# Attention in steps of whole tiles instead of half tiles, ahead of a routed feed-forward layer, on one core

## The chip, the core and the metric

The kernel is one program on one core of a Trainium2 chip. The core has TensorE (matrix products), VectorE, ScalarE, GpSimd and SyncE (here a queue that issues transfers), which run their own instructions in order and wait for each other by semaphores. The metric is device time in microseconds, the median of three runs. One execution was also taken with a profile.

## The reference

Attention over 4 batches of 8 heads, 768 rows, 64 columns a head, feeds a mixture of 8 experts with a fixed capacity and then a two-layer network:

```python
scores = scale * np.matmul(q, k.transpose(0, 1, 3, 2))
is_global = pos[None, :] < n_global              # 8
is_local = (rel >= 0) & (rel < n_local)          # 96
keep = is_global | is_local
dist = np.where(is_global & ~is_local, n_local, np.abs(rel))
scores = np.where(keep, scores - slopes * dist, -1e9)
a = np.exp(scores - scores.max(-1)); a = a / (a.sum(-1) + 1e-9)
x = np.matmul(a, v)      # rows of all heads side by side: 3072 x 512
x = moe(x)               # greedy routing by x @ w_gate, 8 experts of 384 rows
out = (relu-like(x @ w_in)) @ w_out
```

[...]

## The kernel before

The attention goes by 24 tiles of 128 rows (6 to a batch). A tile `g` sees 8 global columns, the 96 before it and its own 128: 232 columns (`KW`); the first tile of a batch sees 128. A tile is worked in two halves of 4 heads, so there are 48 half steps. The order of all instructions is written out by hand, and each engine runs its own in that order. In half step `n` come: the scores of the **next** half (`scores`: 4 products on TensorE; on VectorE the bias and the negative maximum in one instruction a head, L199, called a lift in what follows; on ScalarE the exponential with its sum, L202), the transposes of this half's weights (`transpose_p`: part 0 the own 128 columns, copied to SBUF by VectorE, L217; part 1 the columns before, copied by ScalarE, L215), the combination of the half **two** before (`combine`: a product that turns the values' result back to rows and gives the router's logits, L261, and on VectorE L247, L270, L280, L283), and the values of the half before (`values`, L232, whose result VectorE copies in half 0, L238, and ScalarE in half 1, L236). The columns before a tile end in the tile before, so the values of part 1 are the tile before's `a_v`, into whose first 32 rows GpSimd copies the global values (`place_values`, L177).

Beside this run 32 jobs of `Doubles`, one a half step in four of five (`turn`). A job has raw words of 128x512 weights. *Begin* (at the start of a half step): SyncE issues the load of the job after next (L67), ScalarE makes absolute values (L72) and scales the low words (L74), GpSimd clamps (L73) and then finishes the job before, in every second job with L86 and L87. *Join* (at the end): VectorE shifts (L78) and puts the sign bit in (L79), GpSimd adds the low words (L81). The router's constant tables (`setup`) are made piece by piece, one piece a half step.

After the last `combine` comes the routing of the first expert, then 8 experts on TensorE; that part is the same in both kernels.

Of the kernel before, what the change touches and what calls it, by code (L numbers as in the profile page):

```python
# [30 lines left out]
class Doubles:  # L31
# [58 lines left out]
def attention(ctx, tc, q, k0, k, v, w_gate, n_global, n_local, ident, x_dram, logits, side, router):  # L90
# [43 lines left out]
    vg = consts.tile([C - W, 2, H, D], FT, name="a_vg")  # L134
    pbuf = consts.tile([C, 4, 2, 2 * C], FT, name="a_p")
# [27 lines left out]
    nc.gpsimd.memset(vg, 0.0)  # L163
    nc.gpsimd.memset(cmb, 0.0)
    nc.gpsimd.memset(pbuf[:, :, :, :C - GW], 0.0)
# [7 lines left out]
    def place_values(g, u):  # L173
        b, t = divmod(g, NT)
        if t:
            hs = slice(4 * u, 4 * u + 4)
            nc.gpsimd.tensor_copy(T["v", g - 1][:C - W, hs], vg[:, b % 2, hs])  # L177

    def scores(g, u):
        b, t = divmod(g, NT)  # L180
        if t:
            n, bs = KW, bias
        else:
            n, bs = C, bias0
        ps = [psum.tile([C, 2, KW], FT, name=f"a_s{s}", bufs=2) for s in range(2)]
        if u == 0:
            T["sum", g] = work.tile([C, H], FT, name="a_sum", bufs=3)
            T["mn", g] = work.tile([C, H], FT, name="a_mn", bufs=3)
        for a in range(2):
# [4 lines left out]
        for a in range(2):  # L194
            sx = work.tile([C, 2, KW], FT, name="a_sx", bufs=2)
            pr = T["P", g, 2 * u + a] = pbuf[:, 2 * u + a]
            for s in range(2):
                h = 2 * (2 * u + a) + s
                nc.vector.tensor_tensor_reduce(out=sx[:, s, :n], in0=ps[s][:, a, :n], in1=bs[:, h], scale=-scale,  # L199
                                               scalar=BIG, op0=OP.add, op1=OP.min,  # L200
                                               accum_out=T["mn", g][:, h:h + 1])
                nc.scalar.activation(pr[:, s, 2 * C - n:], sx[:, s, :n], AF.Exp, bias=T["mn", g][:, h:h + 1],  # L202
                                     scale=-1.0, accum_out=T["sum", g][:, h:h + 1])

    def transpose_p(g, u, part):
# [3 lines left out]
        ps = psum.tile([C, 4, C], FT, name=f"a_pt{part}")  # L209
        sb = work.tile([C, 4, C], FT, name=f"a_pts{part}", bufs=2)  # L210
        for i in range(4):
            pr = T["P", g, 2 * u + i // 2][:, i % 2]
            nc.tensor.transpose(ps[:, i], pr[:, :C] if part else pr[:, C:], ident)  # L213
# [4 lines left out]
        T["PT", g, u, part] = sb  # L218

    def values(g, u):  # L220
        t = g % NT
        if g == NG - 1 and u:
            ps = psum.tile([C, 2, KW], FT, name="a_s0", bufs=2)[:, :, :C]
        else:
            ps = psum.tile([C, 2, C], FT, name="a_xp")
# [8 lines left out]
        xt = work.tile([C, 2, C], FT, name="a_xt", bufs=2)  # L234
        if u:
            nc.scalar.activation(xt, ps, AF.Copy)  # L236
        else:
            nc.vector.tensor_copy(xt, ps)  # L238
        T["xt", g, u] = xt

    def divisor(g, u):
        e = T["se", g, u] = work.tile([C, 4], FT, name="a_se", bufs=4)
        nc.gpsimd.tensor_scalar(e, T["sum", g][:, 4 * u:4 * u + 4], 1e-9, None, op0=OP.add)

    def norm(g, u):
        r = T["r", g, u] = rows.tile([C, 4], FT, name="a_r")
        nc.vector.reciprocal(r, T.pop(("se", g, u)))  # L247
# [4 lines left out]
    def combine(g, u):  # L252
        xt = T.pop(("xt", g, u))
# [6 lines left out]
        for a in range(2):  # L260
            nc.tensor.matmul(ps[:, a], xt[:, a], cmb[:, 2 * u + a], start=True, stop=True)  # L261
# [3 lines left out]
        if not last:  # L265
            norm(g, u)
        r = T.pop(("r", g, u))
# [14 lines left out]
        if u:  # L282
            nc.vector.tensor_reduce(logits[:, g, :], T["lp", g].rearrange("c h e -> c e h"), axis=AX.X, op=OP.add)  # L283
            if g < NG - 2:
                T["store"] = g
            else:
                store(g)

    def turn(n):
        return 2 <= n < N - 3 and n % PACE[1] < PACE[0]  # L290

    NG = B * NT
    steps = [(g, u) for g in range(NG) for u in range(2)]
    N = len(steps)
    scores(0, 0)
    setup = router.setup()
    for n in range(N + 2):
        if n < N:
            g, u = steps[n]
            if u == 1 and g + 3 < NG:  # L300
                load_kq(g + 3)
            if u == 1 and g + 2 < NG:
                load_v(g + 2)
            if "store" in T:
                store(T.pop("store"))
            nx = steps[n + 1] if n + 1 < N else None
# [941 lines left out]
```

## Time and profile before

| | us |
|---|---|
| median of 3 runs | 1077.29 (1076.77 to 1078.17) |
| the profiled execution | 1076.5 |
| its span, first to last instruction | 1074.7 |
| TensorE busy in the span | 1032.3 |
| VectorE busy | 739.1 |
| ScalarE busy | 380.3 |
| GpSimd busy | 559.5 |
| mean granted clock of TensorE | 0.986 of full |

A busy time is a share of a span with very different stages: the attention fills the first 197 us, the experts the rest. The granted clock is a share of TensorE's full clock.

### The profile page before, as it was taken

The numbers are of one execution on the slowest core, as the hardware profiler recorded it, in microseconds if no ns is written. First come the engines' busy times: TensorE is split into PE (matmuls) and PEld (weight loads), VectorE is DVE, ScalarE is ACT, GpSimd is POOL, SyncE is SP. The second block draws the span as 40 slices with busy tenths as digits, with TensorE's granted clock in tenths as the row PEclk, the third lists the DMA queues.
The fourth block names the chain that finished last, engine by engine and source line by source line (L and its number), as shares of the span: only waits on it lengthen the run. The fifth ranks groups of instructions, "written<-read, shape, count | busy, mean of one in ns | idle before, by whom it ended". The sixth has DMA issues, their size and how long they took to land.

```text
span 1074.7 us, 19352 instructions
## 1 busy us (share of the span) xinstructions
PE 1032.3 (96%) x6475; PEld 908.8 (85%) x6475; DVE 739.1 (69%) x2215; ACT 380.3 (35%) x958; POOL 559.5 (52%) x867
## 2 busy tenths in 40 slices
PE   8888989789999999999999999999999999999997
PEld 6766767569888988898899888988998999999996
DVE  7999999787878787877887788678855313231322
ACT  6788878233224311331233123312321232124211
POOL 5867876055668434643564346433742464247223
PEclk9999999799999999999999999999999999999999
DMA  8677774152254336335433643543354335335141
GB/s 287 221 243 262 269 268 156 31 150 77 98 193 151 127 109 215 99 109 175 157 93 106 208 136 98 163 151 119 99 175 139 120 124 189 118 118 167 60 136 70
DMA packets 86771, 160.80 MB, mean 150 GB/s; under 512 B 9584, under 2 KB 42864, under 8 KB 86672
## 3 DMA queue, kind: packets, MB, share of 16 engines
q1 hardware_dynamic: 82832, 146.98, 41.3%
q0 software_dynamic: 3840, 12.59, 3.5%
q8 instruction: 51, 0.84, 0.3%
q14 instruction: 48, 0.39, 0.1%
HBM read 138.57 MB, written 20.97 MB: 148 GB/s over the span
## 4 chain that ended last, share of the span: by engine, by line
PE 74%; DVE 6%; POOL 3%; issue 3%; DMA 1%; ACT 1%; POOLq 0%; DVEq 0%; ACTq 0%
PE m_h L983 22%; PE m_acc L1028 22%; PE m_acc L970 12%; PE m_h L943 11%; POOL m_g L912 1%; PE a_xp L232 1%; PE a_pt L213 1%; POOL m_so L912 1%; PE a_s L193 1%; DMA m_x<-x_rows,r_idx 1%; PE m_h L869 1%; ACT a_p L202 1%; DVE r_red L795 1%; PE a_cb L261 1%; DVE a_sx L199 1%
## 5 line engine op out<-in xcount | busy, mean ns | idle before, releaser
L912 POOL TENSOR_TENSOR m_g<-m_t,m_g 128x192 fp32r<-128x192 f32 (+1 forms) x286 | 163.7, 594 | 335.6 <-ACT m_g L992 335.0
L1028 PE MATMUL m_acc<-m_so,m_g 128*128 128x512 f32 x1143 | 294.0, 398 | 0.0
L983 PE MATMUL m_h<-m_y,wi 128*128 128x384 f32 x1536 | 290.1, 339 | 0.0
L983 PEld LDWEIGHTS m_h<-m_y,wi 128*128 128x128 f32 x1536 | 267.4, 188 | 6.6 <-DVE m_xt L885 0.2
L1028 PEld LDWEIGHTS m_acc<-m_so,m_g 128*128 128x128 f32 x1143 | 209.2, 189 | 34.5 <-POOL m_g L912 0.5
L912 POOL TENSOR_TENSOR m_s<-m_r,m_s 128x256 fp32r<-128x256 f32 x256 | 187.3, 755 | 77.5 <-ACT m_s L902 77.2
L992 ACT ACTIVATE m_g<-m_t 128x384 fp32r<-128x384 f32 (+1 forms) x143 | 70.0, 489 | 427.0 <-DVE m_t L991 249.1
L990 DVE TENSOR_SCALAR m_t<-m_h,m_al 128x384 f32<-128x384 f32 (+1 forms) x144 | 82.3, 571 | 155.7 <-PE m_h L983 145.4
L970 PE MATMUL m_acc<-m_hh,m_s 128*128 128x384 f32 x768 | 148.0, 339 | 0.0
L943 PE MATMUL m_h<-m_xt,m_s 128*128 128x384 f32 x768 | 144.4, 336 | 0.6 <-DVE m_xt L885 0.4
L943 PEld LDWEIGHTS m_h<-m_xt,m_s 128*128 128x128 f32 x768 | 134.5, 188 | 2.4 <-DVE m_xt L885 0.6
L970 PEld LDWEIGHTS m_acc<-m_hh,m_s 128*128 128x128 f32 x768 | 132.7, 189 | 0.0
L902 ACT ACTIVATE m_s<-m_r 128x512 fp32r<-128x512 f32 x128 | 79.7, 626 | 68.4 <-PE m_acc L970 66.7
L202 ACT ACTIVATE a_p<-a_sx,a_mn 128x232 f32<-128x232 f32 (+1 forms) x192 | 88.4, 462 | 38.2 <-DVE a_mn L199 38.2
L947 DVE SCALAR_TENSOR_TENSOR m_hh<-m_h,m_hh 128x384 fp32r<-128x384 f32 x64 | 35.5, 555 | 78.4 <-ACT m_hh L946 78.2
L991 DVE SCALAR_TENSOR_TENSOR m_t<-m_h,m_t 128x384 f32<-128x384 f32 (+1 forms) x144 | 73.9, 513 | 4.9
L795 DVE TENSOR_REDUCE r_red<-r_cmp 128x24 bf16<-128x576 bf16 (+1 forms) x97 | 73.8, 761 | 3.3
L213 PE MATMUL a_pt<-ident,a_p 128*128 128x128 f32 x352 | 57.3, 294 | 15.9 <-DVE a_r L247 13.2
L213 PEld LDWEIGHTS a_pt<-ident,a_p 128*128 128x128 f32 x352 | 39.2, 144 | 36.9 <-ACT a_p L202 23.1
L199 DVE CUSTOM_DVE_ANT_0 a_sx<-a_s,a_bias 128x232 f32<-128x232 f32 (+1 forms) x192 | 61.4, 374 | 4.3 <-PE a_s L193 2.6
L946 ACT ACTIVATE m_hh<-m_h 128x384 fp32r<-128x384 f32 x64 | 31.5, 492 | 91.1 <-PE m_h L943 88.8
L193 PE MATMUL a_s<-a_k,a_q 64*128 64x232 f32 (+1 forms) x384 | 51.0, 388 | 3.6 <-DMA a_q<-in_q_dram 3.6
(192 smaller groups left out, 1162.4 us busy)
## 6 DMA issues: line engine op xcount, KB each, us to landing
m_so<-wo_pairs SPq DMA_DIRECT2D x112, 512.0 KB, 3.5
m_r<-in_moe_w_dram SPq DMA_DIRECT2D x128, 256.0 KB, 3.0
a_k<-in_k_dram SPq DMA_DIRECT2D x20, 464.0 KB, 5.2
f_raw<-in_moe_w_in_dram SPq DMA_DIRECT2D x16, 512.0 KB, 4.0
f_raw<-in_moe_w_out_dram SPq DMA_DIRECT2D x16, 512.0 KB, 5.4
wo_pairs<-m_so SPq DMA_DIRECT2D x16, 512.0 KB, 2.7
a_v<-in_v_dram SPq DMA_DIRECT2D x24, 256.0 KB, 5.1
x_rows<-a_xo SPq DMA_DIRECT2D x24, 256.0 KB, 3.0
```

Of the source, the lines that this page charges most:

```text
L199: nc.vector.tensor_tensor_reduce(out=sx[:, s, :n], in0=ps[s][:, a, :n], in1=bs[:, h], scale=-scale, scalar=BIG, op0=OP.add, op1=OP.min, ac ...
L202: nc.scalar.activation(pr[:, s, 2 * C - n:], sx[:, s, :n], AF.Exp, bias=T["mn", g][:, h:h + 1], scale=-1.0, accum_out=T["sum", g][:, h:h + 1])
L213: nc.tensor.transpose(ps[:, i], pr[:, :C] if part else pr[:, C:], ident)
L795: nc.vector.tensor_reduce(red, cmp, axis=AX.X, op=OP.add)
L902: self.nc.scalar.activation(s[:, 0], r, AF.Copy)
L912: self.nc.gpsimd.tensor_tensor(lo[:, c:c + n], x[:, c:c + n], hi[:, c:c + n], op=OP.subtract)
L943: nc.tensor.matmul(ps[:, :n], s1[:, a, d], x[:, b, d], start=(d == 0 and i == 0), stop=(d == self.ND - 1 and i == 2))
L970: nc.tensor.matmul(ps[:, :n], s2[:, b, d * 128:(d + 1) * 128], h[:, a], start=(f == 0 and a + b == 0), stop=(last and a == 1))
L983: nc.tensor.matmul(ps[:, :n], self.wi[:, a, d, f * 128:(f + 1) * 128], y[:, b, d], start=(d == 0 and i == 0), stop=(d == self.ND - 1 and i ...
L990: nc.vector.tensor_scalar(t[:, cs], ps[:, cs], 0.0, self.al[:, f:f + 1], op0=OP.min, op1=OP.mult)
L991: nc.vector.scalar_tensor_tensor(t[:, cs], ps[:, cs], 0.0, t[:, cs], op0=OP.max, op1=OP.add)
L1028: self.nc.tensor.matmul(self.ex[e]["op"][t], g[:, a, t * 128:(t + 1) * 128], s[:, b], start=(f == 0 and a + b == 0), stop=(f == self.F2 // ...
```

## The change

The loop goes by whole tiles. The scores of both halves of the next tile come first on TensorE, then the transposes of half 0, the combination of half 0 of the tile before, the transposes and the combination of half 1, and at the end the values of both halves into one PSUM bank, which ScalarE copies as a whole. The lifts and the exponentials have functions of their own and are spread between. A tile has two begins and two joins as before, at other places, and the divisor and the reciprocal come once a tile. The weights of a tile have their own buffers (`pbuf` by tile), with 232 columns. The 104 values before a tile (global and local) come as an input of their own, `vw`, laid out by the host, so `place_values` goes. In `join` the sign is masked as 16 bits out of the high word and written into the high half of the low word, which the same addition on GpSimd then adds. The router's tables are made only in half steps without a job, and two copies for them go to ScalarE.

```diff
     def join(self, job):
         nc, t = self.nc, job["t"]
+        parts = job["raw"].bitcast(U16).rearrange("p a (b c) -> p a b c", c=2)
         nc.vector.tensor_scalar(t, t, 3, 0x7FFFFFF8, op0=OP.logical_shift_left, op1=OP.bitwise_and)
-        nc.vector.scalar_tensor_tensor(t, job["raw"][:, :, 1], -0x80000000, t, op0=OP.bitwise_and, op1=OP.bitwise_or)
+        nc.vector.tensor_scalar(parts[:, :, 0, 1], parts[:, :, 1, 1], 0x8000, None, op0=OP.bitwise_and)
...
-        x = T["v", g] = loads.tile([C, H, D], FT, name="a_v", bufs=4)
+        x = T["v", g] = loads.tile([C, H, D], FT, name="a_v", bufs=3)
         nc.sync.dma_start(x, v[b, t * C:(t + 1) * C])
-        if not t:
-            nc.sync.dma_start(vg[C - GW:C - W, b % 2], v[b, :G])
+        if t:
+            x = T["vw", g] = loads.tile([GW, H, D], FT, name="a_vw", bufs=3)
+            nc.sync.dma_start(x, vw[b, t - 1])
-    pbuf = consts.tile([C, 4, 2, 2 * C], FT, name="a_p")
+    pbuf = consts.tile([C, 2, NP, 2, KW], FT, name="a_p")
...
+    def lift(g, p):
+        bs = bias if g % NT else bias0
+        sx = T["sx", g, p] = work.tile([C, 2, KW], FT, name="a_sx", bufs=3)
+        for s, ps in enumerate(T.pop(("S", g, p))):
+            h = 2 * p + s
+            nc.vector.tensor_tensor_reduce(out=sx[:, s, :ps.shape[1]], in0=ps, in1=bs[:, h], scale=-scale,
+                                           scalar=BIG, op0=OP.add, op1=OP.min, accum_out=T["mn", g][:, h:h + 1])
...
-            parts.append((T["v", g - 1], T.pop(("PT", g, u, 1))))
+            parts.append((T["vw", g], T.pop(("PT", g, u, 1))))
...
-        xt = work.tile([C, 2, C], FT, name="a_xt", bufs=2)
-        if u:
-            nc.scalar.activation(xt, ps, AF.Copy)
-        else:
-            nc.vector.tensor_copy(xt, ps)
+        if last:
+            nc.scalar.activation(T["xt", g][:, 2 * u:2 * u + 2], ps, AF.Copy)
+        elif u:
+            nc.scalar.activation(T["xt", g], T["xp"], AF.Copy)
...
+    def turn(n, end=False):
+        if 2 <= n < N - 3 and n % PACE[1] < PACE[0]:
+            next(side)
+        elif end:
+            next(setup, None)
...
+    for g in range(NG):
+        n, ahead, prior = 2 * g, g + 1 < NG, g > 0
+        if g + 3 < NG:
+            load_kq(g + 3)
+        if g + 2 < NG:
+            load_v(g + 2)
+        if g > 1:
+            store(g - 2)
+        turn(n)
+        divisor(g)
+        if ahead:
+            scores(g + 1, 0)
+            scores(g + 1, 1)
+            lift(g + 1, 0)
+            expo(g + 1, 0)
+            lift(g + 1, 1)
+            expo(g + 1, 1)
+            lift(g + 1, 2)
+        transpose_p(g, 0, 0)
+        transpose_p(g, 0, 1)
+        if ahead:
+            lift(g + 1, 3)
+            expo(g + 1, 2)
...
+        if prior:
+            combine(g - 1, 0)
+        transpose_p(g, 1, 0)
+        transpose_p(g, 1, 1)
+        turn(n, True)
+        if ahead:
+            expo(g + 1, 3)
+        if prior:
+            combine(g - 1, 1)
+        turn(n + 1)
+        if not ahead:
+            norm(g)
+        values(g, 0)
+        values(g, 1)
+        turn(n + 1, True)
...
-        nc.vector.tensor_copy(self.tp[:, :, 0], first[:, :, None].to_broadcast([128, U, NB, 2]))
-        nc.vector.tensor_copy(self.tp[:, :, 1], inner[:, :, None, None].to_broadcast([128, U, NB, 2]))
+        for k, t in enumerate((first[:, :, None], inner[:, :, None, None])):
+            nc.scalar.activation(self.tp[:, :, k], t.to_broadcast([128, U, NB, 2]), AF.Copy)
```

## Rows read from the trace of the kernel before

**Rows 1.** Stretches: PE, PEld, DVE, ACT, POOL busy; clock, queue share, GB/s.

```profile
61.50:187.30 125.80, 113.81 (x1062) 88.69 (x1063) 120.07 (x469) 104.97 (x345) 93.38 (x134) 0.97 0.71 244
```

**Rows 2.** The join's two lines: duration min/median/max in ns, first and last start.

```profile
L78 DVE TENSOR_SCALAR f_t<-f_t x32: 415/430/1354, 19.9 to 179.0; 128x512 int32<-128x512 int32 x32
...
L79 DVE SCALAR_TENSOR_TENSOR f_t<-f_raw,f_t x32: 691/693/1651, 20.3 to 179.5; 128x512 int32<-128x512 int32 x32
```

**Rows 3.** VectorE in order of time, about a half tile: start, duration, line.

```profile
71.27 0.27 DVE L283 TENSOR_REDUCE logits<-a_lp 128x8 f32<-128x64 f32 x1
71.45 0.42 DVE L238 COPY a_xt<-a_xp 128x256 f32<-128x256 f32 x1
71.78 0.83 DVE L78 TENSOR_SCALAR f_t<-f_t 128x512 int32<-128x512 int32 x1
...
73.25 0.39 DVE L199 CUSTOM_DVE_ANT_0 a_sx<-a_s,a_bias 128x232 f32<-128x232 f32 x1
...
74.53 0.69 DVE L217 COPY a_pts<-a_pt 128x512 f32<-128x512 f32 x1
75.13 0.17 DVE L247 RECIPROCAL a_r<-a_se 128x4 f32<-128x4 f32 x1
75.41 0.19 DVE L270 TENSOR_TENSOR a_lp<-a_cb,a_r 128x32 f32<-128x32 f32 x1
75.51 0.42 DVE L280 TENSOR_TENSOR a_xo<-a_cb,a_r 128x256 f32<-128x256 f32 x1
75.84 0.42 DVE L78 TENSOR_SCALAR f_t<-f_t 128x512 int32<-128x512 int32 x1
76.30 0.77 DVE L79 SCALAR_TENSOR_TENSOR f_t<-f_raw,f_t 128x512 int32<-128x512 int32 x1
```

**Rows 4.** Joins and their hand-over to and from GpSimd, in order of time.

```profile
35.09 0.62 POOL L73 TENSOR_SCALAR f_t<-f_t 128x512 f32<-128x512 f32 x1
...
35.74 0.43 DVE L78 TENSOR_SCALAR f_t<-f_t 128x512 int32<-128x512 int32 x1
...
36.20 0.98 DVE L79 SCALAR_TENSOR_TENSOR f_t<-f_raw,f_t 128x512 int32<-128x512 int32 x1
...
65.00 0.69 DVE L79 SCALAR_TENSOR_TENSOR f_t<-f_raw,f_t 128x512 int32<-128x512 int32 x1
...
65.83 1.28 POOL L81 TENSOR_TENSOR f_t<-f_t,f_raw 128x512 int32<-128x512 int32 x1 [1.62 <-issue]
```

**Rows 5.** The chain that ended last, where TensorE alone sets it.

```profile
168.33 1.02 PE a_pt L213 x8
...
169.84 1.02 PE a_xp L232 x16
170.87 0.98 PE a_s L193 x8
171.85 1.02 PE a_pt L213 x8
```

**Rows 6.** ScalarE in order of time: exponential, copies, first instruction of a begin.

```profile
75.12 0.47 ACT L202 ACTIVATE a_p<-a_sx,a_mn 128x232 f32<-128x232 f32 x1
...
75.59 0.57 ACT L215 ACTIVATE a_pts<-a_pt 128x512 f32<-128x512 f32 x1
76.07 0.36 ACT L236 ACTIVATE a_xt<-a_xp 128x256 f32<-128x256 f32 x1
76.33 0.68 ACT L72 ACTIVATE f_t<-f_raw 128x512 f32<-128x512 f32 x1
```

**Rows 7.** First lift of tiles 2 and 23, and the last values.

```profile
16.78 0.40 DVE L199 CUSTOM_DVE_ANT_0 a_sx<-a_s,a_bias 128x232 f32<-128x232 f32 x1 [0.38 <-PE a_s L193]
...
187.33 0.40 DVE L199 CUSTOM_DVE_ANT_0 a_sx<-a_s,a_bias 128x232 f32<-128x232 f32 x1 [0.50 <-ACT a_xt L236]
...
195.83 1.04 PE L232 MATMUL a_s<-a_pts,a_v 128*64 128x128 f32 x16
```

**Rows 8.** Loads of the raw weights: count, size, median us from issue to landing.

```profile
f_raw<-in_moe_w_out_dram SPq DMA_DIRECT2D x16, 512.0 KB, 5.4
```

More of the change, by code (lines that the diff above doesn't have):

```diff
@@ L171, in attention @@
     load_v(1)
[L173 to L177, printed above, removed]
-    def scores(g, u):
-        b, t = divmod(g, NT)
-        if t:
-            n, bs = KW, bias
-        else:
-            n, bs = C, bias0
-        ps = [psum.tile([C, 2, KW], FT, name=f"a_s{s}", bufs=2) for s in range(2)]
+    def scores(g, u):
+        n = KW if g % NT else C
         if u == 0:
@@ L188, in scores @@
             T["mn", g] = work.tile([C, H], FT, name="a_mn", bufs=3)
+        ps = [psum.tile([C, 2, KW], FT, name=f"a_s{s}", bufs=2) for s in range(2)]
         for a in range(2):
@@ L193, in scores, with expo @@
                 nc.tensor.matmul(ps[s][:, a, :n], T["q", g][r, p], T["k", g][r, p, :n], start=True, stop=True)
[L194 to L203, printed above, removed]
+            T["S", g, p] = [x[:, a, :n] for x in ps]
+    def lift(g, p):
[5 more added lines that the diff above has]
+                                           scalar=BIG, op0=OP.add, op1=OP.min, accum_out=T["mn", g][:, h:h + 1])
+    def expo(g, p):
+        n = KW if g % NT else C
+        sx = T.pop(("sx", g, p))
+        pr = T["P", g, p] = pbuf[:, g % 2, p]
+        for s in range(2):
+            h = 2 * p + s
+            nc.scalar.activation(pr[:, s, KW - n:], sx[:, s, :n], AF.Exp, bias=T["mn", g][:, h:h + 1],
+                                 scale=-1.0, accum_out=T["sum", g][:, h:h + 1])
     def transpose_p(g, u, part):
@@ L283, in combine @@
             nc.vector.tensor_reduce(logits[:, g, :], T["lp", g].rearrange("c h e -> c e h"), axis=AX.X, op=OP.add)
[L284 to L286 removed]
+            if g >= NG - 2:
                 store(g)
[L289 to L290 removed]
+    def turn(n, end=False):
[3 more added lines that the diff above has]
+            next(setup, None)
     NG = B * NT
[L293 removed]
@@ L294, in attention @@
-    N = len(steps)
+    N = 2 * NG
     scores(0, 0)
-    setup = router.setup()
[L297 to L306, printed above, removed]
-            if turn(n):
-                next(side)
-            if nx:
-                scores(*nx)
-            if n == 0:
-                for h in range(H):
-                    slope(bias, rel, h)
-            transpose_p(g, u, 0)
-            transpose_p(g, u, 1)
-            if n == 0:
-                for p in range(NP):
-                    nc.vector.tensor_copy(cmb[:, p, :C], ident)
-            divisor(g, u)
-            if n >= 2:
-                combine(*steps[n - 2])
-        if n == N:
-            norm(*steps[n - 2])
-            norm(*steps[n - 1])
-        if 1 <= n <= N:
-            values(*steps[n - 1])
-        if n == N:
-            router.start()
-            router.early(2)
-        if n >= N:
-            router.early(n - N)
-            combine(*steps[n - 2])
-        if n > N:
-            router.begin(work, lambda: psum.tile([C, 4, C], FT, name="a_pt1").rearrange("c p d -> c (p d)"))
-        if n + 1 < N:
-            place_values(*steps[n + 1])
-        if turn(n):
-            next(side)
-        if n:
-            next(setup, None)
@@ new lines, in attention @@
+    lift(0, 0)
+    lift(0, 1)
+    scores(0, 1)
+    for p in range(NP):
+        if p > 1:
+            lift(0, p)
+        expo(0, p)
+    for h in range(H):
+        slope(bias, rel, h)
+    setup = router.setup()
+    for g in range(NG):
[21 more added lines that the diff above has]
+            expo(g + 1, 2)
+        if not prior:
+            for p in range(NP):
+                nc.vector.tensor_copy(cmb[:, p, :C], ident)
+        if prior:
[9 more added lines that the diff above has]
+        if not ahead:
+            norm(g)
+        values(g, 0)
+        values(g, 1)
+        turn(n + 1, True)
@@ L343 @@
+    router.start()
+    router.early(2)
+    router.early(0)
+    combine(g, 0)
+    router.early(1)
+    combine(g, 1)
+    router.begin(work, lambda: psum.tile([C, 4, C], FT, name="a_pt1").rearrange("c p d -> c (p d)"))
 class Pool:
@@ L1151 @@
     v: bass.AP,
+    vw: bass.AP,
     n_global: int,
```

73 lines of the change are left out of this document (36 added, 37 removed).

## Prediction

> **What bounds the kernel now.** I read the table of stretches first, to see which part of the span the change can touch, then the join's two lines, then VectorE's order of instructions over one tile, then TensorE's and ScalarE's. The attention runs from 0 to about 197 us; all the rest follows it and is not edited, so every gain or loss must come out of those 197 us. In the long even stretch, 61.5 to 187.3 us, VectorE is the fullest engine: 120.07 of 125.80 us. TensorE has 113.81, ScalarE 104.97, GpSimd 93.38 [rows 1]. So VectorE sets the pace and three others stand close behind: a saving on VectorE is worth something only until the next one binds, and only while VectorE need not wait for another engine.
>
> A duration is not yet a price, since instructions of one engine overlap; I take the distance from one start to the next [rows 3]. Four lifts (the score with its bias, line 199) take 1.28, 0.32 each; copying four transposes (L217) 0.60; reciprocal 0.28; logit part (L270) 0.10; the row product (L280) 0.33; the reduction 0.18; the copy of the values (L238) 0.33; L78 0.46. L79 of the join takes 0.69, of which the next start hides 0.08: 0.61. A full tile thus needs 8×0.32 + 2×(0.60 + 0.28 + 0.10 + 0.33) + 0.18 + 0.33 = 5.7 us, and each join 1.07. On top come stretches in which L78 or L79 takes up to 1.35 or 1.65 [rows 2]: the L78 at 71.78 has 0.83 [rows 3].
>
> TensorE: half a tile is 0.98 (scores) + 1.02 (eight transposes) + 0.49 (combine) + 1.02 (values) = 3.51 us, 7.0 a tile [rows 5]. The change removes none of its instructions, so 7.0 is the floor of a full tile.
>
> **The change part by part.**
>
> *Removed from VectorE.* The copy L238, 24 times 0.33: 7.9 us. ScalarE gets it in one copy of 512 columns, which is the shape of L215: 0.48 [rows 6] in place of the 0.26 that it had. One reciprocal a tile goes: 24×0.28 = 6.7. With L79 below (32×0.15) that is 19.4 us. Two copies for the router's table go to ScalarE; they count with the tables.
>
> *L79 becomes a 16-bit instruction with one input.* Nothing before has its shape. From below the nearest row is L78, also one input in SBUF, 512 elements: 0.42, 0.46 to the next start. From above it is the old L79, one element a cycle, with a step of eight bytes on its input: 0.69 and 0.61. I take the lower, because the form (one input, a constant, SBUF to SBUF) is L78's; both ends stay in the range. The Trainium skill (VectorE: DVE Perf Modes, "What auto-detection actually checks") has two elements a cycle for one source with source and destination in SBUF, whatever the step; by it the sum is that of the lower end.
>
> *GpSimd* loses 40 copies of L177 and half of its divisors. It waits more than it works; this is worth nothing by itself, except that L79 is no longer held by L177 (0.69 became 0.77 at 76.30, [rows 3]).
>
> *Tables in quiet slots.* The router's constants are now made only in half-tiles without a join. Those of before lie between joins on VectorE; there they cost their full time.
>
> *Loads.* 20 loads of 104×512 values (0.21 MB each, 4.3 MB) are new, 16 KB ones go. Today's 244 GB/s take 0.71 of the queues [rows 1]; 24 GB/s more make that 0.78. The keys are fetched three tiles ahead and the values two, so I price this at nothing; its cover is that lead. With three buffers for the values instead of four, their load waits in SP's queue for the values of the tile before, which TensorE has done just then; behind it stand the new load, a store and the raw weights of the next job, all with a tile or more to spare but the last (rival D).
>
> *The new order, and the wait that it adds.* This decides. In a tile with two joins VectorE's order is: three pairs of lifts, copy of transposes, fourth pair, combine, copy, **first join**, combine, **second join**. GpSimd ends the first join with L81 (1.28), and only behind it in its order stands L73 (0.62) of the next job, which the second join's L78 needs. L81 starts 0.14 after L79 ends (65.69 to 65.83), and L78 0.03 after L73 (35.71 to 35.74) [rows 4]. Before, half a tile of VectorE work lay between two joins and covered this; now only one combine does (0.10 + 0.33 + 0.18 = 0.6). From the start of the first join's L79 to the second join: 0.43 + 0.14 + 1.28 + 0.1 + 0.62 + 0.03 = 2.60. VectorE's loop over such a tile: 1.92 (lifts) + 0.60 + 0.64 (lifts) + 0.28 + 0.10 + 0.33 + 0.60 + 0.46 (L78) + 2.60 + 0.46 + 0.46 = 8.45 us, of which VectorE stands 1.5 us waiting. TensorE (7.0) and ScalarE are inside: ScalarE has 8×0.47 (exponentials) + 3×0.48 + 4×0.6 (L72, and L74 taken as long) = 7.6 [rows 6]. Behind the waiting L78 stand the next tile's lifts, and behind these the exponentials and the copies that TensorE's transposes wait for.
>
> A tile with only the first join is set by TensorE: 7.0 plus the 0.3 from the first scores to the first lift that its own idle time doesn't cover: 7.3, and the tables fit in. With only the second: from the first lift the exponentials and two copies take 0.4 + 8×0.47 + 2×0.48 = 5.2, then L72 0.7, L73 0.7, L78 and L79 0.9: 7.5. Without joins 7.1.
>
> *The sum.* By the pacing (four of five half-tiles) tiles 3, 6, 8, 10, 13, 15, 16, 18, 20 have two joins and full lifts: 9×8.45 = 76.1. Tiles 5 and 11 too, but the next tile's lifts have 128 columns (0.9 less): 15.1. Tiles 4, 9, 14, 19, 21 have the first join: 36.5. Tiles 1, 2, 7, 12, 17 the second: 37.1 (17 with short lifts). Tile 22: 7.1. GpSimd's L86 falls between L78 and L79 of a second join in eight of them and holds L79 as at 36.20 (0.98 in place of 0.69, [rows 4]): 8×0.3 + 0.8 for the two short tiles = 3.2. Together 175.2 us from the lifts of tile 2 to the end of tile 22's loop.
>
> The lifts of tile 2 start at 16.78 now [rows 7]. In the new order tile 1's scores need not wait for tile 0's transposes; I estimate 15.5. The last tile then has transposes, combine and values of a whole tile after its scores: 5.1 us less the 0.7 by which its scores lie ahead. So the last values end at 15.5 + 175.2 + 4.4 = 195.1, against 195.83 + 1.04 = 196.9 now [rows 7]: 1.8 us. The router's first steps start before the last combine and give about 0.4. The profiled execution took 1076.5 us, span 1074.7; so **1074** (1076.5 − 2.2 = 1074.3). That execution lies 0.8 below the median of 1077.29; I leave this inside the range.
>
> Why so little: 19.4 us of VectorE work leave, and 11 tiles × 1.5 us of new waiting and a longer drain take most of them back.
>
> **Where rule and row are weighed.** L78 takes 0.42 at best and 1.35 at worst [rows 2]; and L79, 0.69 when alone, takes 0.98 at 36.20, where GpSimd has L86 to do behind its L73 [rows 4]. The Trainium skill (SBUF — State Buffer, "Who interferes with whom") says that VectorE in a two-port mode and GpSimd hold a shared port pair for a whole instruction, the second one waiting; the rows agree. By it the new L79, if it runs two elements a cycle, is locked out by every GpSimd instruction and not only by those that read SBUF; here all that run beside it read SBUF, so the sum is the same. Against the change speaks the same skill's Vector Engine (DVE) Microarchitecture Reference, "Measured stream behaviour on trn2": single words apart from each other, not in adjacent pairs, cost a port about 0.65 cycle an element and more. By that the new L79 would be an estimated 0.2 to 0.4 us longer. The old L79 reads words eight bytes apart and still takes 0.69 for 512, one a cycle, so the trace doesn't bear it out on the reading side; writing with such a step no row of VectorE shows.
>
> **The rivals.**
>
> *B, the wait doesn't hold VectorE.* If L73 were through before VectorE got to the second join, the 1.5 us of 11 tiles would be only work, down to TensorE's 7.2: 11×1.25 = 13.8 less, **1060**. For it: today L78 waits for almost nothing. Against: GpSimd works in order, and L81 alone is longer than the combine in front of it. Chance 0.17.
>
> *C, the 16-bit instruction runs one element a cycle* (or pays for its step). Then the first join hands over 0.26 later and the second ends 0.15 later: 11×0.41 + 5×0.15 = 5.3, **1079.6**. For it: its elements lie eight bytes apart. Against: its form. Chance 0.2.
>
> *D, slower: the raw weights come late.* The load of the job after next is issued when L81 of the second join frees its buffer, 1.4 after the first lift; the median of half of these loads is 5.4 us to landing [rows 8], so 6.8; the first L72 of the next tile is due at 7.3, and ScalarE runs in order, so the exponentials stand behind it. ScalarE has about 1 us to give before the copies of the transposes hold TensorE. From landings of some 7.5 us on, each further us costs one per tile with two joins: at 8.3 us, 11×0.8 = 9, **1083**. For it: more bytes, issued as a burst at the tile's start. Against: the queues are not full. Chance 0.15.
>
> *A, the forecast,* 0.48, with its own range 1069 to 1079: hand-overs left out at 0.1 to 0.2 a tile make it 2 to 4 later; L79 held less makes it earlier.
>
> **How the numbers follow.** Under about 0.2% (2.2 us) a measurement can't tell this kernel from itself. Faster: 0.30 of A and all of B, 0.47. Within: 0.15 of A, 0.08 of C, 0.02 of D, 0.25. Slower: 0.03 of A, 0.12 of C, 0.13 of D, 0.28. The range takes in C and most of D, and ends short of B's 1060, so that some 0.18 is left out: 1062 to 1083.
>
> **What the profile after would show.** Right: in tiles with two joins VectorE idles some 1.5 us before the second L78, released by L73, and such tiles come 8.4 to 8.8 apart; the new L79 takes 0.42 to 0.45 when nothing holds it; tiles with one join come 7.2 to 7.6 apart; the last values end near 195. Wrong: tiles of two joins near 7.2 (B); L79 at 0.69 or more (C); L72 waiting for its load (D). Beyond these, a longer first stretch, or a TensorE clock below 0.97 from longer gaps, would make the prediction wrong.

## The result, and the profile after

The changed kernel takes 1082.2 us (median of six, 1081.24 to 1087.55) beside 1076.92 for the one before on the same chip: ratio 1.0057, 95% interval 1.0035 to 1.0079. It is slower by 5 to 6 us; forecast was 1074. The execution that was profiled is the longest of the six, 1087.55 with a span of 1085.8, and had the lowest mean clock of them (0.982, the others 0.983 to 0.988); so the trace holds some 5 us more than the median.

Tiles 7 to 23, from first lift to first lift, as in [rows 1] (the columns are those: PE, PEld, DVE, ACT, POOL, clock, queues' share, GB/s):

```profile
60.20:195.50 135.30, 111.56 (x1080) 93.86 (x1078) 108.48 (x450) 111.12 (x347) 80.50 (x94) 0.95 0.76 258
```

The same tiles took 125.80 before. VectorE did lose work (120.07 to 108.48), GpSimd too (93.38 to 80.50), and the stretch is 9.5 longer: no engine is full any more. A job makes 32-bit floats out of the two 32-bit words of 64-bit weights; its join's two instructions, to hold against [rows 2] (now lines 79 and 80):

```profile
L79 DVE TENSOR_SCALAR f_t<-f_t x32: 416/426/835, 24.6 to 192.1; 128x512 int32<-128x512 int32 x32
its engine sat idle before it (us, times) until:
  POOL f_t L73: 23.4, 15
...
L80 DVE TENSOR_SCALAR f_raw<-f_raw x32: 733/751/1175, 24.9 to 192.4; 128x512 uint16<-128x512 uint16 x32
```

The wait that the forecast named is there, 15 times, 1.6 us on average. VectorE and GpSimd around the second join of a tile (timeline: start, duration, line; in brackets the idle time before it and what ended it):

```profile
81.39 0.42 DVE L79 TENSOR_SCALAR f_t<-f_t 128x512 int32<-128x512 int32 x1
81.72 0.75 DVE L80 TENSOR_SCALAR f_raw<-f_raw 128x512 uint16<-128x512 uint16 x1
82.26 0.23 DVE L270 TENSOR_TENSOR a_lp<-a_cb,a_r 128x32 f32<-128x32 f32 x1
...
84.52 0.43 DVE L79 TENSOR_SCALAR f_t<-f_t 128x512 int32<-128x512 int32 x1 [1.59 <-POOL f_t L73]
84.86 1.16 DVE L80 TENSOR_SCALAR f_raw<-f_raw 128x512 uint16<-128x512 uint16 x1
85.83 0.40 DVE L190 CUSTOM_DVE_ANT_0 a_sx<-a_s,a_bias 128x232 f32<-128x232 f32 x1
...
82.61 1.29 POOL L82 TENSOR_TENSOR f_t<-f_t,f_raw 128x512 int32<-128x512 int32 x1 [2.28 <-ACT a_p L199]
83.87 0.61 POOL L73 TENSOR_SCALAR f_t<-f_t 128x512 f32<-128x512 f32 x1
84.56 0.86 POOL L87 TENSOR_SCALAR wi<-f_t 128x512 fp32r<-128x512 f32 x1
```

Behind the wait, line 80 takes 1.16 instead of 0.75, beside line 87, the first step by which GpSimd finishes every second job. All eight such holds in the trace lie beside it; tiles with two joins and full lifts take 8.93 to 8.95 with a hold and 8.62 to 8.65 without.

What was not forecast stands on TensorE. The next tile has only the first join, and no wait for GpSimd:

```profile
85.36 1.09 PE L211 MATMUL a_pt<-ident,a_p 128*128 128x128 f32 x8
86.29 0.66 PE L261 MATMUL a_cb<-a_cmb,a_xt 128*128 128x144 f32 x4
88.51 1.09 PE L211 MATMUL a_pt<-ident,a_p 128*128 128x128 f32 x8 [1.56 <-DVE a_pts L216]
89.97 0.73 PE L261 MATMUL a_cb<-a_cmb,a_xt 128*128 128x144 f32 x4 [0.37 <-DVE a_xo L280]
90.63 0.44 PE L234 MATMUL a_xp<-a_pts,a_v 128*64 128x128 f32 x4
...
92.54 1.84 PE L182 MATMUL a_s<-a_k,a_q 64*128 64x232 f32 x16
```

TensorE sits idle twice: until VectorE has copied the first transposes (line 216, behind three pairs of lifts), and until VectorE has drained the first combine (line 280, behind all lifts). In [rows 5] its blocks follow each other without a gap. The first lift of the tile after starts at 93.73, 1.19 behind its first score. So the tile is a loop of hand-overs between two engines, 7.9 us long, in which neither is full. TensorE's clock is not what makes it long: the granted clock from 85.83 to 93.73 is 1.00, the 2.4 GHz level.

First lifts of the 24 tiles, read from the trace, split by kind of tile against the forecast's terms:

| | forecast | measured |
|---|---|---|
| first lift of tile 2 | 15.5 | 17.4 |
| 9 tiles with two joins | 78.5 | 78.9 |
| 2 with two joins, short lifts | 15.9 | 16.6 |
| 5 with the first join only | 36.5 | 42.4 |
| 5 with the second join only | 37.1 | 40.2 |
| first lift of tile 23 to the last values | 11.5 | 11.6 |
| last values end | 195.0 | 207.1 |

Before, they ended at 196.9 [rows 7]. The measured column is that of the longest execution.

### The profile page after: what moved, and what is told of

The parts are those of the page before. It is cut to its first block, busy times and chain, and to the rows that moved or that the text cites. A ratio compares the mean times of both kernels' runs of the same rounds, so it can differ in the third digit from the quotient of the medians.

```text
span 1085.8 us, 19053 instructions
## 1 busy us (share of the span) xinstructions
PE 1024.7 (94%) x6475; PEld 913.0 (84%) x6475; DVE 717.2 (66%) x2165; ACT 388.7 (36%) x961; POOL 533.0 (49%) x801
## 4 chain that ended last, share of the span: by engine, by line
PE 73%; DVE 10%; ACT 5%; POOL 5%; issue 5%; DMA 2%; SPq 0%; POOLq 0%; DVEq 0%; ACTq 0%
PE m_h L993 22%; PE m_acc L1038 21%; PE m_acc L980 12%; PE m_h L953 11%; ACT a_p L199 3%; DVE a_sx L190 2%; PE a_xp L234 2%; POOL m_g L922 1%; POOL m_so L922 1%; DVE f_raw L80 1%; DMA m_x<-x_rows,r_idx 1%; PE m_h L879 1%; PE a_cb L261 1%; PE a_s L182 1%; POOL f_t L73 1%
## 5 line engine op out<-in xcount | busy, mean ns | idle before, releaser
L211 PE MATMUL a_pt<-ident,a_p 128*128 128x128 f32 (+1 forms) x352 | 49.9, 282 | 23.4 <-DVE a_pts L216 22.3
L211 PEld LDWEIGHTS a_pt<-ident,a_p 128*128 128x128 f32 (+1 forms) x352 | 37.3, 136 | 35.8 <-DVE a_pts L216 26.2
L182 PE MATMUL a_s<-a_k,a_q 64*128 64x232 f32 (+1 forms) x384 | 45.5, 379 | 6.1 <-DMA a_q<-in_q_dram 5.3
```

The costliest lines, as they stand in the source:

```text
L211: nc.tensor.transpose(ps[:, i], pr[:, :GW] if part else pr[:, GW:], ident)
```

## Experiments

Times are medians, ratios against the kernel before on the same chip. Theories at the start: **W**, the wait for GpSimd's clamp sets the pace; **P**, TensorE's chain does.

**The clamp ahead of the addition.** Each job's begin is issued just before the join of the job ahead of it.

```diff
             yield
+            done, begun = begun, queue.pop(0) if queue else None
             if begun:
-                self.join(begun)
...
+                self.begin(begun)
+            if done:
+                self.join(done)
```

> The changed kernel, with the first half of each job (line 72 to 74) issued just before the join of the job ahead of it instead of after: GpSimd then has the second job's clamp (line 73) ahead of the first join's addition in its order. No work is added or taken away. Theory W (VectorE's 1.6 us waits for GpSimd's clamp, 15 of them, 23.4 us in sum, set the pace of the tiles with two joins): the waits vanish, the 11 tiles with two joins come at the 7.9 us of those with one, 0.7 to 0.9 earlier each, so the time falls by 7 to 10 us, to 1072 to 1075. Rival P (TensorE's chain of transposes, copies and late first lifts sets the pace in all tiles, and VectorE's wait only fills time that it would lose elsewhere): the waits vanish from the list, but the tiles stay at 8.5 or more and the time stays within 3 us, 1079 to 1083.

1083.17, ratio 1.0078 (1.0064 to 1.0091). Three of the waits are left, 2.6 us in sum. Of the nine tiles with two joins and full lifts four come at 8.04 or 8.05 and five at 8.34 to 8.51, instead of 8.62 to 8.95. VectorE at the same place of its order, and GpSimd beside it:

```profile
80.39 0.76 DVE L83 TENSOR_SCALAR f_raw<-f_raw 128x512 uint16<-128x512 uint16 x1
...
81.64 1.51 DVE L82 TENSOR_SCALAR f_t<-f_t 128x512 int32<-128x512 int32 x1
83.07 1.16 DVE L83 TENSOR_SCALAR f_raw<-f_raw 128x512 uint16<-128x512 uint16 x1
...
81.58 1.28 POOL L85 TENSOR_TENSOR f_t<-f_t,f_raw 128x512 int32<-128x512 int32 x1
82.95 0.67 POOL L90 TENSOR_SCALAR wi<-f_t 128x512 fp32r<-128x512 f32 x1
```

The waiting became holding: the second join's first instruction now meets GpSimd's addition for the first join (line 85) and takes 1.51 in place of 0.42. Its second takes 1.16 in place of 0.75 beside line 90, the first step of finishing a job; the four tiles at 8.05 have no such hold. The lifts and copies out of PSUM beside such additions keep their time (0.39 and 0.68 beside the one at 85.89). The hold of the first instruction agrees with the Trainium skill (SBUF — State Buffer, "Who interferes with whom"), by which VectorE in a two-port mode and GpSimd lock one pair of SBUF ports against each other; whether the second runs in such a mode no run here tells. The edit also brought a cost of its own: it needs raw words earlier, and ScalarE waits for four of their loads, 8.8 us in sum. Behind the two longest waits tiles took 11.5 and 10.75, where the changed kernel has 8.02 and 8.54:

```profile
66.29 0.67 ACT L75 ACTIVATE f_t<-f_raw 128x512 f32<-128x512 f32 x1 [3.65 <-DMA f_raw<-in_moe_w_out_dram]
...
110.12 0.68 ACT L75 ACTIVATE f_t<-f_raw 128x512 f32<-128x512 f32 x1 [3.58 <-DMA f_raw<-in_moe_w_out_dram]
```

So the total can't price the wait; the tiles can: of W's 0.7 to 0.9 a tile 0.3 to 0.6 came. Full tiles with the first join only stayed at 7.9, so it is not the wait that makes those long.

**The sign alone, both ways.** In the changed kernel the old instruction back; in the kernel before the new one alone:

```diff
-        nc.vector.tensor_scalar(parts[:, :, 0, 1], parts[:, :, 1, 1], 0x8000, None, op0=OP.bitwise_and)
+        nc.vector.scalar_tensor_tensor(t, job["raw"][:, :, 1], -0x80000000, t, op0=OP.bitwise_and, op1=OP.bitwise_or)
```

> The changed kernel with the old sign instruction back (scalar_tensor_tensor on 32 bits, two inputs) in place of the 16-bit one. From the start of line 79 to the end of the sign the changed kernel takes 0.34 + 0.75 = 1.09 us, the old form 0.46 + 0.69 = 1.15. Theory W (the slowdown is the order and its wait, the 16-bit form is worth almost nothing either way): within 2.5 us of the changed kernel, 1080 to 1085. Rival S (the 16-bit form at one element a cycle is what cost the forecast gain): the old one is clearly better, 1076 to 1079.

> The kernel before with nothing but the 16-bit sign instruction. There VectorE is the fullest engine. By what the changed kernel shows, the pair of join instructions takes 0.34 + 0.53 from start to the next start when nothing holds it, against 0.46 + 0.61: 0.20 less, 32 times, 6.4 us. Theory V (VectorE's work sets the pace before): 3 to 6.5 us faster, 1070.5 to 1074. Rival N (the second instruction, 0.75 in place of 0.69 and still held by GpSimd, gives nothing): 1075.5 to 1078.5.

1088.26 (1.0111, 1.0096 to 1.0127) and 1070.18 (0.9948, 0.9934 to 0.9962). The new form is worth 6 us in either order; for the changed kernel both theories missed that. One instruction got longer (0.75 in place of 0.69) and the pair shorter: from line 79 to 80 it is 0.33, to the next start 0.53, 0.86 in place of 1.07 [rows 3]. The new instruction writes the raw words and not what line 79 has just written.

**Tables alone, laid-out values alone**, each in the kernel before:

> The kernel before with the router's tables alone changed: made only in half-tiles without a join, two copies on ScalarE, in fewer and longer steps. Theory Q (the tables cost VectorE's time where they stand between joins): 1 to 3 us faster, 1074 to 1076. Rival L (the quiet half-tiles are filled by them so that nothing is won, or the longer steps hold the lifts behind them): 1076.5 to 1079.

> The kernel before with the local values laid out by the host alone: the new loads of 104x512 values, no copies on GpSimd, 104 rows in the second transposes, copies and value matmuls, 104 columns in their transposes. The order stays. Theory O (the order is what costs; the loads hide behind their lead of two tiles): within 2 us of the kernel before, or 1 to 2 us faster as VectorE's join is held less, 1074 to 1078. Rival D (4.3 MB more in the queues make raw weights or keys late): 1080 or more.

1072.86 (0.9966, 0.9955 to 0.9977) and 1074.55 (0.9984, 0.9975 to 0.9993). Both gain. So none of these three makes the changed kernel slower; what is left of the change is the order, with the copies of values on ScalarE and one reciprocal a tile.

**The order without joins.** All jobs run behind the loop, in either kernel; only in-loop tiles are compared.

```diff
+    for _ in range(2 * 33 + 2):
+        next(side)
     router.start()
```

> The kernel before with all 32 jobs on the doubles run after the attention's loop instead of in it, so that the tiles show the order alone. The time itself says little, since the jobs then run by themselves. Both theories: tiles at 7.0 to 7.2, set by TensorE, which has 7.0 of work in each.

> The changed kernel with all 32 jobs run after the attention's loop. Theory K2 (the new order's loop of hand-overs through the single buffers of transposes and combines costs by itself): tiles at 7.8 to 7.9, 0.7 more than in the order before. Rival W (the order is as good, only the joins that stand together cost): tiles at 7.0 to 7.3.

Full tiles come 7.05 apart in the old order and 7.89 in the new; from the first lift of tile 2 to that of tile 23 it is 141.3 and 162.3. The windows from tile 5 to tile 22 of the old and of the new order:

```profile
38.50:151.60 113.10, 113.01 (x1154) 92.77 (x1153) 94.98 (x456) 84.03 (x317) 18.40 (x62) 1.00 0.54 182
```

```profile
40.60:171.30 130.70, 115.51 (x1156) 96.94 (x1154) 85.69 (x412) 88.29 (x317) 3.93 (x17) 0.97 0.55 180
```

The old order keeps TensorE busy for 113.01 of 113.10; the new one leaves it idle for 15 us, with every other engine idle more. The order costs 21 us with no join in it. Its 7.89 is not the clock's doing either: from 70 to 95 us, with tiles of 7.89 and 7.90, the granted clock is 1.00. So P holds for tiles with one join or none, and in tiles with two the wait or the hold adds 0.7 to 1.05 to the 7.9.

**Which hand-over?** First the copy of the first transposes ahead of the third pair of lifts:

```diff
-            lift(g + 1, 2)
         transpose_p(g, 0, 0)
         transpose_p(g, 0, 1)
         if ahead:
+            lift(g + 1, 2)
             lift(g + 1, 3)
```

> The changed kernel with VectorE's copy of the first half's transposes (line 216) issued before the third pair of lifts instead of behind it. No instruction is added or taken away. Theory K (a loop of hand-overs sets every tile: scores, 1.19 to the first lift, three pairs of lifts 1.92, the copy 0.6, then only the second half's transposes, which go into the same PSUM buffer, 1.1, combine and hand-over 1.0, values 1.9; 7.9 in all, TensorE idle 1.6 to 1.9 of it): the copy comes 0.64 earlier, tiles with one join or none come at 7.3, 10 tiles by 0.64, so 5 to 7 us less, 1075 to 1077; tiles with two joins stay at 8.6, since their wait for GpSimd is behind the copy, or gain the 0.64 as well (then 1069). Rival X (the pace of those tiles is set by the clock or by ScalarE's exponentials, which get later lifts now): no gain, 1081 to 1084.

1084.34 (1.0077, 1.0057 to 1.0097), tiles at 7.91. TensorE in a tile with one join:

```profile
85.45 0.66 PE L211 MATMUL a_pt<-ident,a_p 128*128 128x128 f32 x4 [0.94 <-DVE a_pts L216]
86.40 0.65 PE L211 MATMUL a_pt<-ident,a_p 128*104 128x128 f32 x4 [0.29 <-ACT a_pts L214]
87.56 0.73 PE L261 MATMUL a_cb<-a_cmb,a_xt 128*128 128x144 f32 x4 [0.51 <-DVE a_xo L280]
```

The copy comes 0.64 earlier, TensorE waits less for it, and then just as long for the next thing: the second combine has to wait until line 280 has emptied the one buffer of the combines, which is behind the same eight lifts, copy and reciprocal in either order. By that reading the loop has two ends of equal length, and one was moved. The time is rival X's, but the cause is not the clock: the granted clock from 83.41 to 91.32, the tile of these rows, is 1.00.

**The joins apart**, the second one behind the next tile's third pair of lifts; and **both**:

```diff
             lift(g + 1, 2)
+        if prior:
+            turn(n - 1, True)
+        turn(n)
```

> The changed kernel with the second join of a tile moved behind the next tile's third pair of lifts, so that some 2.5 us of VectorE's work out of PSUM lie between any two joins; the first half of the next job follows it. No work is added or taken away. The run with the next job begun ahead showed that without the wait for the clamp the second join is held just as long (1.51 and 1.16 in place of 0.42 and 0.75) while GpSimd adds the first. Theory W2 (two joins 0.7 apart cost VectorE some 1.6, as a wait or as a held instruction, whatever GpSimd's order): waits and held instructions are gone, tiles with two joins come at the 7.9 of the hand-over loop, or at 8.7 less 0.8: 11 times, 1072 to 1075. Rival K alone (the loop of hand-overs, into which the second join moves with its 0.87, since it now stands between the scores and the copy of the transposes): 1081 or more.

> Both together: the copy of the first transposes behind the second pair of lifts, then the second join of the tile before, then the third and fourth pair. Theory K with W2: the loop of hand-overs is 7.3 in all tiles, and VectorE has 7.1 of work in those of two joins, so 7.3 to 7.6 a tile: against the changed kernel's sum from tile 2 to the end some 17 to 25 us less, 1057 to 1065. If only W2 holds: 1072 to 1075. If only K: 1075 to 1077. If neither: 1081.

1089.06 (1.0109, 1.0094 to 1.0124) and 1099.41 (1.0197, 1.0171 to 1.0224). In the first, which came as rival K alone had it, VectorE never waits for the clamp, and most joins are not held (medians 0.42 and 0.74; nine of the 64 instructions are, up to 1.52 and 1.83, the longest beside GpSimd's other steps). Undisturbed full tiles with two joins take 8.67 to 8.71: the 7.89 of the loop and most of the 0.86 of the join that now stands in it, between the scores and the copy for which TensorE waits. Three tiles took 10.1 to 10.4, at a granted clock of 0.71 and 0.84, so the total holds more than the moved join. VectorE has time enough; it lies elsewhere, in front of the lifts (view of waits, 17 to 190 us):

```profile
DVE a_sx L190 <- PE a_s L182: 35.6, 20, 3.4
```

In the second, with copy and join both in the loop, tiles took up to 10.99, with TensorE at a granted clock of 0.83 from 74 to 105 us.

**Scores by pairs**, each pair's lift written behind its products:

```diff
             scores(g + 1, 0)
+            lift(g + 1, 0)
             scores(g + 1, 1)
-            lift(g + 1, 0)
             expo(g + 1, 0)
             lift(g + 1, 1)
+            scores(g + 1, 2)
             expo(g + 1, 1)
             lift(g + 1, 2)
+            scores(g + 1, 3)
```

> The changed kernel with the scores written pair by pair in the program, each pair's lift written right behind its two matmuls; TensorE's own order stays. Theory F (the first lift waits for all four matmuls of a half because the wait is taken from the order in the program, 1.19 where one pair would be 0.7): the lifts start 0.4 to 0.5 earlier in tiles that the loop of hand-overs sets, 5 to 9 us less, 1073 to 1077. Rival B (the four matmuls share a buffer, and the second pair now waits for the first pair's lift): TensorE gets 0.4 or more of wait in each half, 1085 to 1100.

1145.55 (1.065, 1.0628 to 1.0671). Rival B, and worse than it said:

```profile
PEld a_s L183 <- DVE a_mn L191: 42.3, 33, 2.4
```

Two pairs share a buffer, and the products of the second wait until VectorE has read the first. The Trainium skill (PSUM — Partial Sum Buffer, "PSUM bank collisions raise a hardware error") asks for such a guard, as TensorE must not write a bank that another engine reads; no run here lets the two meet. So, with two pairs in a buffer, an earlier lift is paid for by later products, and this order did not give the 1.19 back. From 60 to 250 us the granted clock is 0.84, so some of the loss is the clock's.

**Values ahead of the second combine**, with the copy first; once with the jobs, once with them behind the loop:

```diff
-        if prior:
-            combine(g - 1, 1)
         turn(n + 1)
...
         values(g, 0)
         values(g, 1)
+        if prior:
+            combine(g - 1, 1)
```

> The changed kernel with the copy of the first transposes behind the second pair of lifts, and with the values of a tile issued ahead of the second combine of the tile before (the second job's first half stays where it was, ahead of the values). No work is added or taken away. With the copy alone the tiles stayed at 7.9, since the wait went over to the second combine: it waits for the row product of the first (line 280), out of the one buffer of the combines, behind all eight lifts. Theory K2 (the loop scores, first lift 1.19, all lifts with copy, reciprocal and product 3.9, second combine 0.7, values 1.9, 7.9 in all, is what sets tiles with one join): with the values ahead, TensorE has work where it waited, tiles with one join come at 7.3 to 7.5; the second join stands 2 us behind the first, so GpSimd is through and tiles with two joins come at 7.7: 11 times 0.9 and 10 times 0.5, 15 us less, 1065 to 1070. Rival C2 (TensorE's clock, which falls in more tiles than before, and not the loop, makes the tiles long): 1079 to 1083. Rival J (the drain of the second combine is now late, the next lifts stand behind it and behind the second join): 1082 or more.

> The changed kernel with all jobs behind the attention's loop, and in the loop the copy of the first transposes behind the second pair of lifts and the values ahead of the second combine. To be compared with the run of the changed order without jobs, which has 7.89 a full tile and 1194.15. Theory K2 (TensorE waits in a loop of hand-overs through the single buffers; with work in between it has none left): full tiles at 7.05 to 7.3, 10 to 15 us less, 1179 to 1184. Rival (another hand-over of the same length stands behind it, as the last combine's drain in front of the next lifts): 7.6 to 7.9, 1189 or more.

Without jobs full tiles fell from 7.89 to 7.55, and the time from 1194.15 to 1189.49: so the loop ran through this hand-over, but undoing it pays only 0.34 of the 0.84, since the last combine's drain now stands right in front of the next lifts (VectorE waits 1.88 for it). With the jobs the time rose to 1091.0 (1.014, 1.0115 to 1.0164): two tiles with the first join only came down to 7.57 and 7.58, those with two joins stayed at 8.6 or more, and several took 9.4 or 10.4. One of these on TensorE:

```profile
80.69 0.66 PE L211 MATMUL a_pt<-ident,a_p 128*128 128x128 f32 x4 [1.39 <-DVE a_pts L216]
81.70 0.65 PE L211 MATMUL a_pt<-ident,a_p 128*104 128x128 f32 x4 [0.35 <-ACT a_pts L214]
82.28 0.44 PE L234 MATMUL a_xp<-a_pts,a_v 128*64 128x128 f32 x4
...
84.00 0.64 PE L234 MATMUL a_xp<-a_pts,a_vw 104*64 104x128 f32 x4
```

Behind two idle stretches the same products take 0.64 in place of 0.39; the granted clock of that tile is 0.84, and 0.50, the 1.2 GHz level, from 84 to 86 us.

**The parts without the order.** Sign, tables and laid-out values together in the old order; then with every copy of values on ScalarE, as the change has it:

```diff
-        if u:
-            nc.scalar.activation(xt, ps, AF.Copy)
-        else:
-            nc.vector.tensor_copy(xt, ps)
+        nc.scalar.activation(xt, ps, AF.Copy)
```

> The kernel before with the 16-bit sign, the tables apart and the local values laid out together; its order by half-tiles stays. Alone the three gave 6.3 (0.52%), 3.7 (0.34%) and 1.8 us (0.16%). Theory O (these parts are gains on VectorE's path that add up, and the order by whole tiles alone makes the changed kernel slower): 1064 to 1067. Rival S (they win the same time, since behind VectorE TensorE stands close): 1068 to 1071.

> The same with the copy of every half-tile's values on ScalarE, as the change has it, in place of every second one on VectorE. It takes 24 times 0.33, 7.9 us, from VectorE and gives 24 times 0.38, 9.1, to ScalarE, which had 105 busy of 126 in the long stretch. Theory V (VectorE still sets the pace): 3 to 8 us less than without it, 1058 to 1062. Rival A (ScalarE runs in order and does the copies behind the exponentials, so the combines get their values later): no gain or a loss, 1064 to 1070.

1068.23 (0.9924, 0.9911 to 0.9938) and 1066.37 (0.9907, 0.9889 to 0.9924). Faster than either kernel, but short of the sum; that the copies on ScalarE gain is not clear of the intervals here. Both lose time near 18 us, as does the run with the laid-out values alone (10.56 from tile 2 to tile 3, where the kernel before has 7.47). ScalarE in the first and in the second, and the windows of 4 us behind it in the second:

```profile
18.46 0.67 ACT L72 ACTIVATE f_t<-f_raw 128x512 f32<-128x512 f32 x1 [2.45 <-DMA f_raw<-in_moe_w_in_dram]
```

```profile
20.57 0.66 ACT L72 ACTIVATE f_t<-f_raw 128x512 f32<-128x512 f32 x1 [4.46 <-DMA f_raw<-in_moe_w_in_dram]
```

```profile
18.00:22.00 4.00, 1.41 (x16) 0.87 (x12) 0.81 (x5) 1.43 (x3) 0.61 (x1) 0.97 1.05 344
22.00:26.00 4.00, 3.70 (x12) 2.44 (x12) 3.00 (x12) 4.00 (x17) 3.78 (x4) 0.50 0.87 327
```

The queues are full there (1.05), the first raw words are late, TensorE stands (2.89 before line 207 at 22.30), and then runs at half its clock (0.50, the 1.2 GHz level). Last, the first two of these loads are issued ahead of the fourth tile's keys:

```diff
     setup = router.setup()
+    next(side)
     for n in range(N + 2):
...
-            if turn(n):
+            if n > 2 and turn(n):
                 next(side)
```

> The three parts in the order before, with the first two loads of raw weights issued ahead of the fourth tile's keys and queries and the third tile's values instead of behind them. Theory L (the parts' gain is eaten at the start, where the laid-out values make the first raw weights late and TensorE's clock falls behind the stall): the wait of 2.5 us near 18 us goes, tile 3 starts 3 us earlier, 1064 to 1066. Rival (the later loads are then late instead, so the stall moves to the fourth tile): 1067 to 1069.

> The same with the copies of the values all on ScalarE. Theory L: the wait of 4.5 us and the clock's fall behind it go, tile 3 starts 5 to 6 us earlier, 1060 to 1062. Rival: the stall moves on, 1065 to 1067.

1067.11 (0.992, 0.9907 to 0.9934) and 1063.3 (0.9884, 0.9868 to 0.9899). The stall and the fall of the clock are gone in both, but they gave back 1.1 us, which lies within the intervals, and 3.1, at their edge; theory L had more. In the first, tile 3 starts 2.8 earlier and 2.0 of it are lost again by tile 23, at tile 3 (8.54 in place of 7.47) and tile 20 (7.90 in place of 7.02). The kernel before takes 8.39 and 7.91 there; why the run with the stall is shorter at these two is open. Between these two runs the copies on ScalarE gain 3.8 us, clear of the intervals. The second is the best version here, 12.4 us under the kernel before: all of the change but its order and the divisor and reciprocal by whole tiles, with two loads moved.

## Why the prediction was wrong

- **The step that failed** is "7.0 is the floor of a full tile", and with it "A tile with only the first join is set by TensorE: 7.0 plus the 0.3". It summed each engine's work, took TensorE's as the time of a tile, and left the hand-overs out at "0.1 to 0.2 a tile". In the new order 7.0 was not reached: with no join at all a full tile takes 7.89, with the clock at 1.00, where the old order takes 7.05. [Rows 5] show TensorE without gaps in an order where the values' inputs were drained half a tile earlier and two pairs of lifts stand ahead of each copy of transposes; the new one puts three or four pairs of lifts between a product and the drain that frees its buffer. Tiles with one join missed by 0.6 and more, 9.0 of the 12.1 us by which the last values missed the forecast (42.4 and 40.2 in place of 36.5 and 37.1); some 3 of the 9.0 are two tiles in which the clock fell, and this execution is some 5 us longer than the median. That the single buffers close the loop is read from TensorE's waits and from the two ends that were moved (7.91 and 7.55 a tile); no run gave the transposes or the combines a second buffer.
- **First lift.** No row stands behind the 0.3 from the first scores to the first lift. The lift starts 1.19 behind its first score, in the kernel before too (16.78 [rows 7], the score at 15.59), and this is a part of the loop.
- **The start**, 15.5, was an estimate: 17.4, later than before. Ahead of tile 2's scores, tile 0's transposes and values waited 0.88 and 0.47 for VectorE's copies, the same hand-over.
- **Tiles with two joins** were nearly right, 8.45 and 8.75 against 8.62 to 8.95, and so was the wait with its place and length. But it is not what makes the kernel slower than the one before, as I would have said: such tiles took 8.8 on average there as well, 8.6 without one of 11.4, and 8.7 here. With the next job begun ahead they came at 8.04 to 8.51, the nearer to the loop's 7.9 the less they were held.
- **The 16-bit instruction** takes 0.75, not 0.43, so rival C was right about it. Which of its two reasons holds, one element a cycle or a price for the step, is open. C's price of 5.3 us was wrong all the same: the instruction doesn't need what the one ahead of it writes and starts 0.33 behind it, so the pair costs 0.86, less than the 0.92 that I took. The rule of the Trainium skill that stands for the lower end (VectorE: DVE Perf Modes, "What auto-detection actually checks") is not borne out here. The one set against it (Vector Engine (DVE) Microarchitecture Reference, "Measured stream behaviour on trn2") gave an estimated 0.2 to 0.4 more, and 0.33 came. The 0.69 of the old L79 lies nearly as close, so this doesn't prove the reason.
- **Loads at nothing**: right in the even stretch and wrong at the start in the old order, where they made the first raw words late. Rival D is real (the early begin and the parts' start show it) but is not what happened to the changed kernel: ScalarE waited 0.4 for its raw words there.
- **The clock.** I named a lower clock from longer gaps as what could make it wrong. It is 0.95 in place of 0.97 over the long stretch; two tiles with the first join only, 9.17 and 9.51, hold such a fall (granted clock 0.81 and 0.82). What it costs the median was not measured by itself.

Of the 1082 then: in the old order the parts give 1068, and 1066 with the copies on ScalarE, so the order by whole tiles, with one divisor and one reciprocal a tile, takes back some 14 to 16 us. Without joins it costs 0.84 a full tile, 21 us from tile 2 to tile 23; with them the tiles with one join pay it, and those with two are about as long as before.

## What to carry to other kernels

The fullest engine's work is not yet the floor of a stage; the longest loop of hand-overs can stand above it. Follow one buffer from the product that fills it to the instruction that empties it and ask what stands ahead of that one in its engine's order; with single buffers that distance can become idle time. Moving one end of such a loop can uncover the next of equal length, so test an order with the side work taken out before pricing the side work. And run the parts of a change apart: four gains and one loss looked like one small loss.

## What the runs showed of the hardware

- A 16-bit operation on 512 halves that lie eight bytes apart, on both sides in SBUF, takes 0.73 to 0.76 us when nothing holds it, where one on 512 whole words in a row takes 0.42; behind an instruction of 0.42 on which it doesn't depend, it starts 0.33 after that one's start.
- VectorE's instructions from SBUF to SBUF are held beside GpSimd's: line 82 of the early begin took 1.51 (for 0.42) beside an addition of 1.28, line 83 1.16 (for 0.75) beside line 90. In the kernel before with the sign alone the second took 1.83 at 76.50, beside the subtraction by which GpSimd finishes a job (line 88, 1.36 from 76.36). Lifts and copies out of PSUM kept their time beside the addition.
- TensorE's granted clock fell to 0.50 (22 to 26 us) behind a wait of 2.89, in the parts with all copies on ScalarE, and to 0.50 (84 to 86 us; 0.84 over the tile) behind gaps of 1.39 and 0.35, in the run with the values first; there the products took 0.64 in place of 0.39.
